# A gated linear attention and MLP kernel: four batches side by side on partition quarters, 32x32 transposes on VectorE, and an order of issue set by hand

## The chip, the cores and the metric

The kernel runs on one core of a Trainium2 chip. The metric is the device time of one execution in microseconds (us), as a median over runs. Engines: PE is TensorE, PEld its weight loads, DVE is VectorE, ACT is ScalarE, POOL is GpSimd, SP is the engine whose queue issues most DMAs.

## The reference

Four batches, eight heads, 768 tokens, 48 dimensions per head, in float32. A gated linear attention is followed by an MLP with a SoLU activation and a layer norm:

```python
for t in range(S):
    state = alpha[:, :, t, :, None] * state + einsum('bhd,bhe->bhde', k[:, :, t], v[:, :, t])
    y[:, :, t] = einsum('bhd,bhde->bhe', q[:, :, t], state)
x = y.transpose(0, 2, 1, 3).reshape(B * S, H * D)          # 3072 x 384
h = x @ w_in                                                # 3072 x 1024
e = exp(h - h.max(-1));  sm = e / (e.sum(-1) + 1e-9)
solu = h * sm
ln = (solu - mean) / sqrt(var + 1e-6) * g_ln
out = ln @ w_out                                            # 3072 x 384
```

The weights arrive as float64, and the kernel converts them to float32 itself.

## The kernel before

Both kernels cut the tokens into chunks of 128, 24 in all. In each chunk the decays become products by two scans along time (one backward for the keys, one forward for the queries). For that alpha, q and k must lie with the dimensions on the partitions and time along the row. The old kernel transposes them on PE, two heads to a matmul, and ACT copies the result out:

```python
    def transposed(src, dst):
        tp = ps_tp.tile([P, NP, P], FP, tag="tp", name="tp")
        for j in range(NP):
            nc.tensor.transpose(out=tp[:, j], in_=src[:, 2 * j : 2 * j + 2, :], identity=ident)
        nc.scalar.copy(out=dst, in_=tp)
```

The scores of a chunk are 8 matmuls with 48 rows each, in two row strips. What is read from the state and what comes from the scores are summed in four column strips of 32:

```python
        for j in range(NP):
            for i in range(2):
                nc.tensor.matmul(a[i][:, j], lhsT=d["kT"][heads[i], j], rhs=d["qT"][heads[i], j], ...)
        # ... reading the state, h being the head, r the column strip
        mm(a, r, states[b][:, h // 2, h % 2], d["qT"][:, h // 2])
```

The loop issues one chunk of attention, one up-projection (`up`, two halves, with exp on ACT and the product on DVE after each) and one output projection (`down`) in every round. The order of its instructions on each engine is not the order of the text: a scheduler moves them.

The fast path must prove that the weights were in range. So both kernels fetch the weights a second time, one piece a chunk, and ACT takes sums of it:

```python
    def in_range(i):
        raw = fetch(i)                                   # DMA, on SP's queue
        sq = wtmp.tile([P, raw.shape[1]], FP, tag="sq", name="sq")
        nc.scalar.activation(out=sq, in_=raw[:, :, 1].bitcast(FP), func=AF.Square, accum_out=far[:, i, 0:1])
        nc.scalar.activation(out=sq, in_=sq, func=AF.Exp, scale=-(2.0**24), accum_out=far[:, i, 1:2])
```

## Time and profile before

| | before |
|---|---|
| time, median of 3 runs | 464.62 us (464.06 to 465.41) |
| span of the profiled run, granted PE clock | 462.2 us, 0.971 |
| PE busy | 90% |
| first output projection starts | 96.5 us |
| one period on PE (one chunk) | 16.74 us, so 66.9 for four |

The prediction below shows the lines that carry this.

### The profile page before, as it was taken

The page shows a single profiled execution, that of the slowest core. Times are in us where ns is not written, and L with a number is a line of the kernel's source. Part 1 is how long each engine was busy: PE and PEld are TensorE (multiplying, and loading weights), DVE is VectorE, ACT ScalarE, POOL GpSimd, SP SyncE. Part 2 cuts the span into 40 slices and gives each one's busy share as a digit, 9 for nine tenths or more (in the row PEclk, how much of TensorE's full clock was granted, in tenths as well). Part 3 has the DMA queues.
Part 4 walks back from the last instruction along what each step waited for, and adds up shares of the span by engine and source line. Part 5 has one row for each costly group of instructions (what it writes and reads, how often), then busy time and mean ns, then how long its engine had stood idle before and what let it go on. Part 6 is the DMA issues. An engine that isn't in the chain of part 4 may idle for free.

```text
span 462.2 us, 9424 instructions
## 1 busy us (share of the span) xinstructions
PE 416.6 (90%) x3827; PEld 341.2 (74%) x3827; DVE 278.0 (60%) x562; ACT 161.9 (35%) x320; POOL 198.8 (43%) x212
## 2 busy tenths in 40 slices
PE   2546848889999999999999999999999999999992
PEld 2336737668878877977987887887797798778761
DVE  5738979996655654764754755665576475454121
ACT  3122335424434538613423332332241242333210
POOL 8435646755334424433524533443442453443120
PEclk9996986999999999999999999999999999999997
DMA  8696449145445549332341332333231100000001
GB/s 185 172 186 152 92 107 178 37 87 132 114 79 118 111 91 272 101 70 36 71 81 27 77 74 47 59 70 70 36 70 34 18 18 18 13 8 19 18 17 43
DMA packets 133477, 37.02 MB, mean 80 GB/s; under 512 B 126504, under 2 KB 129840, under 8 KB 133424
## 3 DMA queue, kind: packets, MB, share of 16 engines
q1 hardware_dynamic: 133120, 36.19, 36.2%
q8 instruction: 32, 0.52, 0.5%
q14 instruction: 21, 0.17, 0.1%
q10 hardware_dynamic: 304, 0.14, 0.1%
HBM read 31.59 MB, written 4.72 MB: 79 GB/s over the span
## 4 chain that ended last, share of the span: by engine, by line
PE 80%; DVE 11%; POOL 6%; issue 1%; ACT 1%; DMA 0%; SPq 0%; POOLq 0%; DVEq 0%; ACTq 0%
PE o L306 27%; PE h L274 26%; PE y L216 7%; PE tp L127 7%; PE a L190 5%; PE kv L248 4%; POOL low L406 2%; PE tp_k L203 2%; PE o L301 2%; DVE top L402 2%; DVE qF L151 1%; DVE power L405 1%; DVE top L399 1%; DVE sT L195 1%; DVE hT L141 1%; DVE w_out L408 1%
## 5 line engine op out<-in xcount | busy, mean ns | idle before, releaser
L274 PE MATMUL h<-xT,w_in 128*128 128x128 f32 x1152 | 141.3, 279 | 12.5 <-POOL w_in L408 7.2
L274 PEld LDWEIGHTS h<-xT,w_in 128*128 128x128 f32 x1152 | 135.9, 195 | 15.0 <-POOL w_in L408 7.8
L306 PE MATMUL o<-w_out,u 128*128 128x385 f32 x384 | 130.7, 492 | 0.9 <-POOL w_out L444 0.5
L306 PEld LDWEIGHTS o<-w_out,u 128*128 128x128 f32 x384 | 70.9, 190 | 46.6 <-DVE w_out L444 1.5
L327 POOL TENSOR_TENSOR r<-sums,mhalf 128x1 f32<-128x1 f32 x24 | 13.2, 551 | 127.7 <-DVE sums L323 127.7
L128 ACT COPY aT<-tp 128x512 f32<-128x512 f32 x24 | 14.0, 585 | 129.6 <-PE tp L127 129.6
L316 DVE COPY sums<-o 128x3 f32<-128x3 f32 x24 | 3.9, 161 | 90.5 <-PE o L306 90.4
L280 DVE TENSOR_TENSOR u<-h,e 128x512 f32<-128x512 f32 x48 | 32.9, 685 | 41.4 <-ACT e L279 41.3
L162 POOL TENSOR_TENSOR qT<-qT,qF 128x512 f32<-128x512 f32 x24 | 28.5, 1188 | 46.5 <-DVE qF L151 41.0
L281 ACT ACTIVATE u<-u 128x512 f32<-128x512 f32 x48 | 30.2, 630 | 48.4 <-DVE u L280 48.4
L279 ACT ACTIVATE e<-h 128x512 f32<-128x512 f32 x48 | 28.6, 596 | 50.1 <-PE h L274 49.7
L289 POOL TENSOR_TENSOR part_e<-e 128x512 f32<-128x512 f32 x24 | 31.2, 1299 | 19.3 <-ACT e L279 19.3
L216 PE MATMUL y<-sT,vn 128*32 128x128 f32 x768 | 29.2, 285 | 11.1 <-DVE sT L195 11.1
L169 POOL TENSOR_TENSOR kT<-kT,hT 128x508 f32<-128x508 f32 x24 | 28.5, 1189 | 17.3 <-ACT kT L128 17.1
L141 DVE TENSOR_TENSOR_SCAN hT<-aT,unit 128x516 f32<-128x516 f32 x24 | 29.6, 1232 | 8.3 <-ACT aT L128 8.2
L190 PE MATMUL a<-qT,kT 48*128 48x128 f32 x384 | 28.8, 291 | 5.9 <-POOL qT L162 5.6
L216 PEld LDWEIGHTS y<-sT,vn 128*32 128x32 f32 x768 | 22.9, 115 | 13.7 <-DVE sT L195 13.3
L195 DVE TENSOR_TENSOR sT<-a,mask 128x512 f32<-128x512 f32 x48 | 30.8, 680 | 0.9 <-PE a L190 0.8
L151 DVE TENSOR_TENSOR_SCAN qF<-aT,seed 128x516 f32<-128x516 f32 x24 | 30.2, 1259 | 1.2 <-DVE seed L149 0.5
L190 PEld LDWEIGHTS a<-qT,kT 48*128 48x128 f32 x384 | 24.1, 193 | 8.9 <-POOL qT L162 5.7
L292 POOL TENSOR_TENSOR part_e<-part_e 128x256 f32<-128x256 f32 x24 | 27.7, 1154 | 1.9
L289 DVE TENSOR_TENSOR part_u<-u 128x512 f32<-128x512 f32 x24 | 18.9, 787 | 15.4 <-ACT u L281 15.4
(85 smaller groups left out, 544.7 us busy)
## 6 DMA issues: line engine op xcount, KB each, us to landing
raw<-in_moe_w_out_dram SPq DMA_DIRECT2D x16, 384.0 KB, 3.9
an<-in_alpha_dram SPq DMA_DIRECT2D x24, 192.0 KB, 2.7
qn<-in_q_dram SPq DMA_DIRECT2D x24, 192.0 KB, 3.3
kn<-in_k_dram SPq DMA_DIRECT2D x24, 192.0 KB, 3.0
out_dram<-o_sb SPq DMA_DIRECT2D x24, 192.0 KB, 2.1
raw<-in_moe_w_in_dram SPq DMA_DIRECT2D x32, 128.0 KB, 3.2
vn<-in_v_dram SPq DMA_DIRECT2D x24, 128.0 KB, 2.5
raw<-in_moe_w_in_dram SPq DMA_DIRECT2D x32, 64.0 KB, 2.7
```

What stands on the lines that cost most here:

```text
L127: nc.tensor.transpose(out=tp[:, j], in_=src[:, 2 * j : 2 * j + 2, :], identity=ident)
L141: nc.vector.tensor_tensor_scan(out=h[:, 0 : NP * SW][:, ::-1], data0=a.rearrange("p j s -> p (j s)")[:, ::-1], data1=unit.rearrange("p j s ...
L151: nc.vector.tensor_tensor_scan(out=d["qF"].rearrange("p j s -> p (j s)"), data0=a.rearrange("p j s -> p (j s)"), data1=s.rearrange("p j s ...
L190: nc.tensor.matmul(a[i][:, j], lhsT=d["kT"][heads[i], j], rhs=d["qT"][heads[i], j], start=True, stop=True)
L195: nc.vector.tensor_tensor(out=d["sT"][:, i], in0=a[i], in1=mask[:, None, :].to_broadcast([P, NP, P]), op=ALU.mult)
L216: nc.tensor.matmul(y[32 * r : 32 * r + 32, a], lhsT=lhsT, rhs=rhs, start=r not in begun, stop=stop, skip_group_check=True, tile_position=( ...
L274: nc.tensor.matmul(h[:, f], lhsT=w_in[:, a, (f0 + f) * P : (f0 + f + 1) * P], rhs=d["xT"][:, a], start=(a == 0), stop=(a == KC - 1),)
L279: nc.scalar.activation(out=d["e"][:, fs], in_=h, func=AF.Exp)
L280: nc.vector.tensor_tensor(out=d["u"][:, fs], in0=h, in1=d["e"][:, fs], op=ALU.mult)
L281: nc.scalar.activation(out=d["u2"][:, fs], in_=d["u"][:, fs], func=AF.Square)
L289: eng.tensor_tensor(out=t, in0=d[key][:, 0:HF], in1=d[key][:, HF:FC], op=ALU.add)
L306: nc.tensor.matmul(o[:, 0 : DM + 1], lhsT=d["u"][:, f], rhs=w_out[:, f], start=(f == 0), stop=(f == FC - 1), skip_group_check=True,)
```

## The change

The intent is to give PE less attention work. One chunk of each of the four batches is done at the same time, each batch on a quarter of the partitions. So there are six groups of four chunks. alpha, q and k are loaded so that DVE's 32x32 transpose finishes them with no matmul and no copy; scores run in four row strips, the state is read with 32x32 tiles in all 16 positions. The diff, cut to its core:

```diff
+    ctx.enter_context(tc.manual_schedule())
...
-    def transposed(src, dst):            # PE and ACT
...
+    def load(g):
+        for src, dst in ((alpha, an), (k, kn), (q, qn)):
+            for b in range(B):
+                nc.sync.dma_start(
+                    out=dst[32 * b : 32 * b + 32].rearrange("t h u d -> t h (u d)"),
+                    in_=src[b, :, t, :].rearrange("h (t u) d -> t h (u d)", u=TQ))
+    def blocks(src, dst, extra):
+        nc.vector.transpose(out=dst.rearrange("p h (t u) -> p h u t", u=TQ), in_=src[:, :, :, 0:E0])
+        nc.vector.transpose(out=extra.rearrange("p j (i t u) -> p u j i t", u=TQ, i=2), in_=...)
...
+    def scores(g, half):
+        for i in range(NP):
+            h = half * NP + i
+            for kb, qb in ((h, h), (H + h // 2, H + h)):
+                for b in range(B):
+                    nc.tensor.matmul(a[b][:, i], lhsT=kT[quarter(b), kb], rhs=qv[quarter(b), qb],
+                                     tile_position=(32 * b, 0), ...)
+    # reading the state
+    mm(b, a, r, 32 * b, state[p, rows + h, e], qv[p, rows + h])        # tile_position=(32 * b, 32 * r)
...
     for m in range(N + DOWN):
+        g, s = m // B + 1, m % B
+            if s == 0:
+                alpha_T(g)
+                for i in range(3):
+                    scan_back(g, i)
+            elif s == 1:
+                for i in range(3):
+                    scan_on(g, i)
         if rise:
             up(m, 0)
         if m > DOWN:
             finish(m - DOWN - 1)
+            s == 0: keys_T, keys, alpha_max, decay      s == 1: queries_T, queries, load(g + 1)
+            s == 2: scores(g, 0)                        s == 3: keys_back(g)
+        if m < DOWN: ... bits(i); add(i)                # conversion of w_out
         if rise:
             up(m, 1)
             partial(m)
+        if attn and s == 3: read_out(g)
         if fall:
             down(m - DOWN)
+        if attn and s == 2: scores(g, 1)
+        if attn and s == 3: next_state(g); load_v(g + 1)
+        if 0 <= m - 6 < len(pieces):
+            in_range(m - 6)
```

`manual_schedule` turns the scheduler off, so every engine now runs its instructions in the order of this text.

## The prediction

> **What bounds the kernel now.** I read the page's busy shares and its slices first, then the chain that ended last, then one period of TensorE's timeline.
>
> ```profile
> PE 416.6 (90%) x3827; PEld 341.2 (74%) x3827; DVE 278.0 (60%) x562; ACT 161.9 (35%) x320; POOL 198.8 (43%) x212
> ...
> PE   2546848889999999999999999999999999999992
> ...
> DVE  5738979996655654764754755665576475454121
> ...
> PEclk9996986999999999999999999999999999999997
> ...
> PE 80%; DVE 11%; POOL 6%; issue 1%; ACT 1%; DMA 0%; SPq 0%; POOLq 0%; DVEq 0%; ACTq 0%
> ```
>
> There are two stages. In the first eight or so slices (11.6 us each) PE is partly idle and DVE is nearly full; from then on PE is full to the end. The chain says the same: PE holds 80% of it, and the DVE and POOL shares are weight conversion and scans at the start. The merged chain in order of time gives the border: the first row below is the first output projection, the second the last one.
>
> ```profile
> 96.49 4.80 PE o L306 x14
> ...
> 448.48 5.31 PE o L306 x16
> ```
>
> So 96.5 us of prologue, about 357 us in which PE sets the pace, and a tail of 8.4 us after 453.8. One period of the steady part, on PE (start, length, line, operation):
>
> ```profile
> 302.29 0.60 PE L127 MATMUL tp<-ident,an 128*128 128x128 f32 x4
> 302.72 0.60 PE L127 MATMUL tp<-ident,qn 128*128 128x128 f32 x4
> 303.16 2.84 PE L274 MATMUL h<-xT,w_in 128*128 128x128 f32 x24
> 305.93 1.16 PE L190 MATMUL a<-qT,kT 48*128 48x128 f32 x16
> 307.02 0.66 PE L127 MATMUL tp<-ident,kn 128*128 128x128 f32 x4
> 307.52 2.84 PE L274 MATMUL h<-xT,w_in 128*128 128x128 f32 x24
> 310.20 0.60 PE L203 MATMUL tp_k<-ident,kT 128*128 128x128 f32 x4
> 310.73 0.86 PE L216 MATMUL y<-qT,state 128*32 128x128 f32 x24
> 311.41 1.06 PE L216 MATMUL y<-sT,vn 128*32 128x128 f32 x32
> 312.39 1.16 PE L248 MATMUL kv<-vn,kg 128*128 128x128 f32 x8
> 313.39 0.28 PE L301 MATMUL o<-ones,sum_e 128*128 128x1 f32 x2
> 313.53 0.36 PE L301 MATMUL o<-ones,sum_u 128*128 128x1 f32 x2
> ```
>
> No row waits for another engine, so a row costs the distance from its start to the next start (the printed lengths overlap). The chain's rows put one period at 16.74 us (320.06 less 303.32). The parts: up-projection 2 x 2.68 = 5.36; output projection 5.29 and its sums 0.36, together 5.65; attention 5.65, of which transposes 0.43 + 0.44 + 0.50 + 0.53 = 1.90, scores 1.09, reading the state 0.68, scores times values 0.98, new state 1.00. Check of this ledger: from 96.5 us the old kernel has 24 output projections (135.6), 21 up-projections (112.6) and 20 chunks of attention (113, less 4 new states never made) to do: 96.5 + 357.2 = 453.7, and the trace has 453.8.
>
> The 24 passes that read the state take 0.68 us, 28 ns each, against 2.68/24 = 112 ns for a pass that fills the array: four column strips run side by side at nearly full gain. The scores use two row strips: 16 in 1.09 us, 68 ns each.
>
> **What the Trainium skill says.** "TensorEngine Tiling (Array Packing)", section Tiling Modes, has 32-row, 32-column and 32x32 tiles run independently, with a drain when the mode changes; the 28 ns and 68 ns agree. "TensorE: Matmul & The Clock Gate", Part 3, gives 10.6 times for 16 tiles, and a few ns from tile to tile; nothing in this trace has 16 tiles. "Vector Engine (DVE) Microarchitecture Reference", section 3.8, sustains one element per cycle per lane in the 32x32 transpose; no transpose of DVE is in this trace. "SBUF — State Buffer", section "SBUF: two separate sides", has DVE and GpSimd exclude each other on a shared port pair. The trace agrees: the same small operation takes 0.16 us when POOL is quiet and 0.82 us when it starts after a POOL operation.
>
> ```profile
> 9.79 0.16 DVE L148 TENSOR_SCALAR least<-hT 128x4 f32<-128x4 f32 x1
> ...
> 305.01 0.82 DVE L148 TENSOR_SCALAR least<-hT 128x4 f32<-128x4 f32 x1
> ...
> 304.98 0.83 POOL L181 TENSOR_TENSOR state<-state,hT 128x384 f32<-128x384 f32 x1 [1.11 <-DVE hT L141]
> ```
>
> **The change part by part, on PE.** The new kernel works in six groups of four chunks (one chunk of each batch). Each matmul is two passes. Per group:
> - Transposes of alpha, q and k leave PE: 4 x 1.37 = 5.5 us. The keys' way back needs 12 transposes where there were 16: 12 x 0.11 + 0.1 = 1.45, before 2.1.
> - Scores: a head's 48 dimensions become 32 and a masked 16, so 64 matmuls, 128 passes. Four row strips at once: 32 rounds of 0.112 = 3.6, with starts 3.9; before 4.4.
> - Reading the state: 128 matmuls of 32x32, 256 passes. In 16 tiles that is 16 rounds of 0.112 = 1.8, estimate 1.9; before 2.7.
> - Scores times values: the same 128 passes in four strips, 32 x 0.11 = 3.5, with starts 3.7; before 3.9.
> - New state: 32 matmuls of 64 columns and 16 of 128, four strips: 16 x 0.056 + 8 x 0.11 = 1.8, estimate 2.0; before 4.0.
> Sum 13.0 us a group against 22.6: 2.4 us less per chunk. A chunk then costs 5.36 + 5.65 + 3.2 = 14.3 us where it cost 16.7, if PE never waits.
>
> **On the other engines.** ACT loses three copies of 0.58 us per chunk. DVE gains six transposes per group, 1024 or 512 elements a lane, an estimate of 1.07 and 0.53 us from the page above, some 5.2 us a group with overheads; it saves a quarter of the scans (six of 1.23 us per group where there were eight) and small state additions. Steady DVE work is near 40 us of a 57 us group: enough on average. But DVE and POOL now do a group's preparation in one lump. The chunks of a group: the first carries alpha's transposes, three backward scans, the keys; the second three forward scans, the queries; the third issues the scores, first half, right after its first up-projection. DVE, from the group's start to the end of the query transposes: state 1.4, alpha 1.8, scans 3.7, keys 1.7, maximum 1.7, up-projection products 3 x 0.69, finishing 2 x 0.64, partial sums 2.0, forward scans with their small operations 7.0, queries 1.7, in all 24.4; POOL then needs 1.2 + 2.4 for the queries: 28 us. PE gets there after two chunks and one up-half, 2 x 11.0 + 2.7 = 24.7. A wait of about 3.4 us a group; without collisions on the shared port (partial 1.35, forward scans 5.2) about 1, with all of them about 6. Four groups (2 to 5) have it in the steady part.
>
> **Prologue.** Here DVE sets the end. Its work up to the last scores of group 1: transposes 10.4, twelve scans 14.8, their small operations 5, maxima 3.4, weight conversion 36 (six pieces of 0.42 + 1.30 + 0.58 us, eight of 0.51 + 0.87 + 0.62, half the additions), sixteen masks at 0.68 = 10.9, products and partial sums 10.2, state 1.1: 92 us. It starts when alpha has landed, about 6.5 us (0.79 MB at the 185 GB/s of the first slice plus 2.7 us), and loses some 5 us while group 0 goes around DVE, POOL and PE: 104. Then PE reads group 1 out (5.6), forms the mean of the output weights (16 passes, 5.2) and waits for the first subtraction (1.5): first output projection at about 116, not 96.5, but with one more up-projection and four more chunks of attention behind it. If conversion runs without collisions it is near 106.
>
> **Sum.** After that: 24 output projections 135.6, 20 up-projections 107.2, attention of groups 2 to 4 3 x 13.0, of the last group without state update 9.5, new state of group 1 2.0, changes of mode and gaps 3, in all 296. With a first projection at 112 (between 106 and 116), waits of 4 x 2.5 = 10 (I take less than 3.4, since an order set by hand was probably tried), and the tail 8.4: 426.4 of span. The time is 2.4 us more than the span before (464.6 against 462.2): 428.8, given as 428.
>
> **The rivals.**
> 1. DVE becomes the bound. For: 92 us in the prologue, 24 in two chunks of 22. Against: 40 of 57 over the group. If its transposes run at half rate, 5 us a group are added in the prologue and before the scores: 10 + 4 x 5 = 30, so 455.
> 2. The 16 tiles don't run side by side, because each pass has its own weight load (PEld is 74% busy). At the 28 ns of four strips the state costs 7.2 in place of 1.9 a group; five groups: +26, so 454. For: nothing here has more than four tiles. Against: starts in a strip group follow within nanoseconds, loads included.
> 3. Nothing waits and the prologue is short: 106 + 296 + 8.4 + 2.4 = 413.
> 4. The transposes' share was hidden and nothing is gained. Against: PE's rows show no wait, and the ledger closes within 0.1 us, so a microsecond off PE is one off the time.
>
> **Range and chances.** Low 408: rival 3 and a little from the prologue. High 450: rivals 1 or 2 nearly in full. For less than 2% gain (above 455.3) both would have to come, or a stall I don't see: faster 0.93, same 0.05, slower 0.02.
>
> **What would show it.** PE's period over four chunks should be 57 to 62 us (66.9 before). The timeline should have no transposes from an, qn or kn; the state's 256 passes in about 2 us, the scores' 128 in about 3.9. The first output projection should start at 106 to 118. A wait of PE's first score of a group for POOL's queries should stand at 1 to 6 us. DVE's 128x1024 transpose should take about 1.1 us. I am wrong if the state's passes stay near 28 ns, if the transposes take 2 us, or if PE waits for DVE at the up-projections too.

## More of the kernel before

One more line helps to compare later. It is the busy time of every engine in a stretch of time (columns: stretch, its length, busy us and instructions of PE, PEld, DVE, ACT, POOL, then granted clock, DMA share, GB/s):

```profile
21.00:96.50 75.50, 51.35 (x407) 43.32 (x407) 61.56 (x103) 27.76 (x52) 43.97 (x39) 0.86 0.58 120
```

Between the first up-projection and the first output projection DVE is busy 61.6 of 75.5 us, 82%.

## The result, and the profile after

The kernel after takes 546.17 us (median of 4 runs, 545.51 to 549.36); before takes 464.34 in the same rounds. The ratio is 1.1765, 95% interval 1.1708 to 1.1822. The result is correct. The prediction of a gain was wrong: the kernel lost 18%.

Busy shares, slices and the chain by engine on the page of the kernel after:

```profile
PE 405.8 (74%) x5007; PEld 329.8 (60%) x5007; DVE 292.1 (53%) x479; ACT 128.6 (23%) x251; POOL 173.2 (32%) x169
...
PE   0028527366899599987689895698796888999993
...
DVE  2998879574159764059624156716245864033411
...
PEclk9999966586989979998888998987999979899997
...
PE 41%; DVE 25%; DMA 12%; POOL 6%; ACT 5%; issue 5%; SPq 4%; DVEq 0%; ACTq 0%; POOLq 0%
```

PE's busy time went down only from 416.6 to 405.8 us, at least in part because some of it ran at a lower clock (0.901 over the run, before 0.971). More important, no engine is full any more. PE has holes from end to end, DVE swings between 9 and 0, and PE holds 41% of the chain where it held 80%. A kernel in which nobody is full and the chain hops among four engines and the DMA queues is bound by waiting.

The chain's rows for the first and the last output projection:

```profile
151.87 7.14 PE o L327 x16
...
533.86 5.31 PE o L327 x16
```

The prologue is 151.9 us (before 96.5, predicted 112), and the stretch after it is 547.6 - 151.9 = 395.7 us (predicted 426.4 - 112 = 314.4). So of the 121 us by which the span missed, 40 lie before the first output projection and 81 after it. One group took 85.1 us, from the up-projection that starts at 232.57 to the one at 317.69.

PE's waits, summed (columns: who waits, for whom, us in total, times, longest):

```profile
PE a L216 <- POOL qv L192: 47.4, 6, 29.1
PE h L295 <- DVE u L301: 45.2, 14, 10.5
PE y L240 <- issue: 12.3, 9, 1.8
PE tp L229 <- DVE sT L221: 11.2, 2, 9.7
```

The wait for the queries (first line) was predicted: apart from one of 29 us at the very start it is 18.3 us in five groups (2.0 us in group 1, 4.1 in each of groups 2 to 5). The second line was not: PE stands 14 times at the up-projection for DVE's product `u`. DVE is only 53% busy, so why is the product late? The merged timeline of all engines answers for one of those places:

```profile
238.40 5.43 PE L327 MATMUL o<-w_out,u 128*128 128x385 f32 x16
239.21 2.19 SPq L385 DMA_DIRECT2D raw<-in_moe_w_in_dram  x4
243.94 0.66 ACT L435 ACTIVATE sq<-raw 128x512 f32<-128x512 f32 x1 [18.52 <-DMA raw<-in_moe_w_in_dram]
...
245.35 0.58 ACT L300 ACTIVATE e<-h 128x512 f32<-128x512 f32 x1
245.97 0.69 DVE L301 TENSOR_TENSOR u<-h,e 128x512 f32<-128x512 f32 x1 [6.31 <-ACT e L300]
...
246.71 0.71 PE L295 MATMUL h<-xT,w_in 128*128 128x128 f32 x4 [2.88 <-DVE u L301]
```

Read it backwards. PE waits 2.88 us for `u`; DVE has waited 6.31 us for the exponential `e`; the up-projection behind `e` had ended at 238, but ACT stood 18.52 us at `sq`, the first instruction of the range check, until its weight piece landed. "Perfetto Trace Analysis", section Tensor Engine Instruction, of the Trainium skill says that ACT, DVE and GpSimd are strict FIFOs; this trace agrees, `e` stood 7 us behind `sq`. And the fetch itself was late: it is issued at 239.21, behind the value loads on SP's queue, which had to wait for their buffer. A little later the same queue shows another such order, with twelve loads ahead of the piece (SP's DMA issues):

```profile
265.24 1.89 SPq L124 DMA_DIRECT2D an<-in_alpha_dram  x4
267.17 3.33 SPq L124 DMA_DIRECT2D kn<-in_k_dram  x4
270.60 2.31 SPq L124 DMA_DIRECT2D qn<-in_q_dram  x4
273.54 3.28 SPq L385 DMA_DIRECT2D raw<-in_moe_w_in_dram  x4
```

A wait could also cost more than its own length. Here are the same 64 score matmuls twice (columns as in the windows above): first a half that PE began without a wait, then the half that began after 4.10 us of waiting for the queries.

```profile
204.80:206.80 2.00, 2.00 (x66) 1.88 (x65) 0.00 (x0) 0.66 (x2) 0.00 (x0) 1.00 0.00 0
269.94:273.67 3.73, 3.73 (x64) 3.50 (x64) 2.35 (x4) 0.63 (x1) 2.88 (x3) 0.50 1.12 203
```

After the wait the granted clock reads 0.50 in place of 1.00, and the matmuls take 3.73 us in place of 2.0. Not every wait did this: the 24 up-projection matmuls that began at 246.71 after 2.88 us of waiting took 2.94 us, about as long as those that began at 296.21 without a wait (2.84).

The transposes took twice what was predicted (groups by form; us in total, mean ns):

```profile
L137 DVE STREAM_TRANSPOSE kT<-kn 128x1024 f32<-128x1024 f32 x6 | 12.3, 2050 | 0.7 <-DMA kn<-in_k_dram 0.6
...
L138 DVE STREAM_TRANSPOSE kT<-kn 128x512 f32<-128x512 f32 x6 | 6.5, 1088 | 0.0
```

And PE's read-out of group 3 with its holes:

```profile
299.82 2.24 PE L240 MATMUL y<-qv,state 32*32 32x128 f32 x150
303.53 1.58 PE L240 MATMUL y<-qv,state 32*32 32x128 f32 x102 [1.47 <-issue]
305.04 1.06 PE L240 MATMUL y<-sT,vn 128*32 128x128 f32 x26
306.98 3.04 PE L240 MATMUL y<-sT,vn 128*32 128x128 f32 x102 [0.88 <-issue]
```

Two holes of 1.47 and 0.88 us are put down to "issue": nothing that the profile shows was missing. Some 0.9 and 1.5 us before the holes begin, at about 301.2 and 304.6 us, the instruction queue moved a packet of 16 KB. Without the hole the first two rows take 2.24 + 1.51 = 3.75 us for 252 of the 256 passes that read the state, where I had predicted 1.9.

### The profile page after: what moved, and what is told of

It reads as the page before. It is cut to its first block, busy times and chain, and to the rows that moved or that the text cites. A ratio compares the mean times of both kernels' runs of the same rounds, so it can differ in the third digit from the quotient of the medians.

```text
span 547.6 us, 11453 instructions
## 1 busy us (share of the span) xinstructions
PE 405.8 (74%) x5007; PEld 329.8 (60%) x5007; DVE 292.1 (53%) x479; ACT 128.6 (23%) x251; POOL 173.2 (32%) x169
## 3 DMA queue, kind: packets, MB, share of 16 engines
q10 hardware_dynamic: 1088, 1.71, 1.6%
## 4 chain that ended last, share of the span: by engine, by line
PE 41%; DVE 25%; DMA 12%; POOL 6%; ACT 5%; issue 5%; SPq 4%; DVEq 0%; ACTq 0%; POOLq 0%
PE o L327 14%; PE h L295 12%; PE y L240 7%; PE a L216 4%; DMA kn<-in_k_dram 4%; DVE aT L157 3%; DMA raw<-in_moe_w_in_dram 3%; DVE u L301 3%; DVE qv L137 2%; DMA raw<-in_moe_w_out_dram 2%; DMA an<-in_alpha_dram 2%; DVE kT L137 2%; POOL low L410 2%; DVE sT L221 2%; PE kv L274 1%
## 5 line engine op out<-in xcount | busy, mean ns | idle before, releaser
L295 PE MATMUL h<-xT,w_in 128*128 128x128 f32 x1152 | 155.0, 299 | 45.2 <-DVE u L301 45.2
L295 PEld LDWEIGHTS h<-xT,w_in 128*128 128x128 f32 x1152 | 149.2, 213 | 55.1 <-DVE u L301 51.0
L216 PE MATMUL a<-qv,kT 32*128 32x128 f32 x768 | 45.3, 383 | 55.5 <-POOL qv L192 47.4
L216 PEld LDWEIGHTS a<-qv,kT 32*128 32x128 f32 x768 | 40.9, 282 | 60.5 <-POOL qv L192 48.6
L283 DVE TENSOR_TENSOR state<-state,kv 128x512 f32<-128x512 f32 x8 | 5.5, 688 | 46.8 <-PE kv L274 46.8
L179 POOL TENSOR_TENSOR kT<-kT,hT 128x1016 f32<-128x1016 f32 (+1 forms) x12 | 20.0, 1689 | 32.0 <-DVE kT L137 32.0
L435 ACT ACTIVATE sq<-raw 128x384 f32<-128x384 f32 (+1 forms) x14 | 8.4, 599 | 86.6 <-DMA raw<-in_moe_w_in_dram 56.9
L240 PE MATMUL y<-qv,state 32*32 32x128 f32 x1280 | 21.5, 278 | 8.1 <-issue 7.9
L240 PEld LDWEIGHTS y<-sT,vn 128*32 128x32 f32 x768 | 22.6, 115 | 6.9 <-issue 6.7
L157 DVE TENSOR_TENSOR_SCAN aT<-aT,seed 128x516 f32<-128x516 f32 x18 | 24.2, 1346 | 0.6
L410 POOL TENSOR_TENSOR low<-low,power 128x384 f32<-128x384 f32 (+1 forms) x14 | 16.2, 1156 | 24.6 <-DVE power L409 15.3
```

The costliest lines, as they stand in the source:

```text
L157: nc.vector.tensor_tensor_scan(out=o, data0=a, data1=s, initial=1.0, op0=ALU.mult, op1=ALU.add)
L216: nc.tensor.matmul(a[b][:, i], lhsT=kT[quarter(b), kb], rhs=qv[quarter(b), qb], start=kb == h, stop=kb != h, tile_position=(32 * b, 0), sk ...
L240: nc.tensor.matmul(y[b][quarter(r), a], lhsT=lhsT, rhs=rhs, start=(b, r) not in begun, stop=stop, tile_position=(row, 32 * r), skip_group_ ...
L295: nc.tensor.matmul(h[:, f], lhsT=w_in[:, a, (f0 + f) * P : (f0 + f + 1) * P], rhs=d["xT"][:, a], start=(a == 0), stop=(a == KC - 1),)
L410: nc.gpsimd.tensor_tensor(out=low, in0=low, in1=power.bitcast(FP), op=ALU.mult)
```

## The experiments

There were 15 runs. The time of the kernel before on the same chip stands beside each result. Runs e1 to e11 are single executions, so their state is unknown; differences under 2 us are not read from them (the kernel before was between 465.0 and 466.3 beside them). The four runs of e12 spread over 4.4 us and those of e15 over 3.2, so the 5 us of e5 and of e9 below are little more than such a spread. e12 to e15 were timed in three rounds. Results are correct unless said otherwise.

### e1 and e2: the range check

e1 leaves the check out (and sets its sums to zero). e2 keeps it, but fetches the piece two chunks before ACT reads it:

```diff
-        if 0 <= m - 6 < len(pieces):
-            in_range(m - 6)
+        if float64 and 0 <= m - 6 < len(pieces):
+            fetch(m - 6, nc.sync)
+        if 0 <= m - 8 < len(pieces):
+            in_range(m - 8)          # without its own fetch
```

> The weight-range checks (14 pieces fetched once more and squared on ACT) are left out, nothing else. Theory A (ACT works in order of issue; a check waits there for its piece, whose transfer stands on the SP queue behind the loads of the next group, and the exponentials behind the check are late, so PE waits): a group of four chunks falls from 85 to 62-68 us, the time from 546 to 470-490 us. Rival B (DVE's slower transposes, 2.05 us in place of 1.07, and the lump of preparation set the group): the group stays above 78 us and the time above 520.

> All checks are made, but each stands on ACT two chunks after its transfer was issued; the transfers stand where they stood. Theory A: within 8 us of e1_nocheck, 470-495 us, with no wait of ACT for a piece over 2 us. If it is the work or the bytes of the checks and not the waiting: near 546.

e1 took 515.31 us and e2 514.23 (before 466.28). So the check costs 31 to 32 us by its waiting and nothing by its work: with all the work kept, but the data there in time, the same 32 us are won. The direction was right, the size too large: e1 lies between what the two theories expected. In e2 a group takes 71.2 us instead of 85.1. The first output projection stays at 152.8: all of this lies after it.

### e3 and e4: the scheduler

e3 takes the `manual_schedule` line out of the kernel after. e4 puts the same line into the kernel before.

```diff
-    ctx.enter_context(tc.manual_schedule())      # e3, from the kernel after
+    ctx.enter_context(tc.manual_schedule())      # e4, into the kernel before
```

> The same program without the hand-set order: the scheduler orders each engine's instructions as it does in the kernel before. Theory A and its twin in the prologue (conversions at ACT's head): 430-480 us, first output projection before 125 us. If the layout itself is what costs (slow transposes, preparation in lumps): above 510.

> The kernel before, with its program order as the order of issue. If an order fixed by hand is costly wherever a check or conversion is waited for at an engine's head: 490-560 us against 464. If the hand order is harmless by itself and only this layout suffers: within 15 us of 464.

e3 took 478.09 and e4 498.98 (before 466.28). One line is worth 68 us in the new kernel: of the 80 us lost (against the 466.28 of these rounds), 68 are the order and 12 the rest. All of the 68 lie after the first output projection: that stretch is 320.7 us in e3 and 395.7 in the kernel after, while the prologue did not get shorter (155.6 and 151.9). It is no fault of the new order alone, because the old kernel's text, run as it is written, also loses 33. PE's waits in e4:

```profile
PE kv L249 <- ACT kg L206: 51.8, 19, 17.8
PE tp L128 <- DMA an<-in_alpha_dram: 20.5, 2, 16.1
```

There the copy of the keys stands in ACT's queue behind a square that waits for DVE, and PE waits for it nearly once a chunk. The scheduler had hidden this. Of the 33 us, 24 lie before the first output projection (at 120.5 us, where it was 96.5). In e3 a group takes 62.7 us, well under the 66.9 of before; what the new layout loses there lies in the prologue (first output projection at 155.6).

### e5: the transposes alone

e5 is e3 with the transposes writing side by side instead of 16 bytes apart. The result is wrong (time order is scrambled), the work is the same.

```diff
-        nc.vector.transpose(out=dst.rearrange("p h (t u) -> p h u t", u=TQ), ...)
+        nc.vector.transpose(out=dst.rearrange("p h (u t) -> p h u t", u=TQ), ...)
```

> The scheduled form of e3_auto, with the transposes' output written contiguously within a block (the order of positions is wrong, so the result is wrong on purpose). If the 16-byte step of the output is what makes a 128x1024 transpose take 2.05 us: 1.1 us each, and the time falls from 478 to 455-468. If the transpose of 4-byte elements runs at half rate whatever the output: 2.0 us and 474-480 us.

```profile
L136 DVE STREAM_TRANSPOSE kT<-kn 128x1024 f32<-128x1024 f32 x6 | 7.4, 1235 | 0.1
...
L137 DVE STREAM_TRANSPOSE kT<-kn 128x512 f32<-128x512 f32 x6 | 4.0, 669 | 0.0
```

The 1024-element transpose goes from 2.05 to 1.24 us and the 512-element one from 1.09 to 0.67. From the two sizes, an element costs (1235 - 669)/512 = 1.1 ns side by side and (2050 - 1088)/512 = 1.9 ns at a step of 16 bytes. The time was 472.66 (before 465.29), only 5.4 us under e3: the output step is the cause of the slow transposes, but in that order of issue slow transposes were no large part of the loss.

### e6: the next group's first DVE work earlier

In the order by hand, alpha's transposes and the three backward scans stood at the start of a group, ahead of the product that PE needs. e6 is e2 with this lump issued at the end of the group before.

```diff
+    def early(g):
+        alpha_T(g)
+        for i in range(3):
+            scan_back(g, i)
...
-            if s == 0:
-                alpha_T(g)
-                for i in range(3):
-                    scan_back(g, i)
...
             up(m, 1)
             partial(m)
+            if attn and s == 3 and g + 1 < G:
+                early(g + 1)
```

> e2_checklate, with the alpha transposes and backward scans of the next group moved to the last chunk of the group before, where DVE is idle. Theory C (the lump of DVE work in a group's first two chunks makes PE wait for the queries, 4.1 us, and the products, 1.7 us): those two waits go, PE's clock stays up in between, the group falls from 71.2 to 62-66 us, the time from 514 to 485-495. If DVE's lump is not it: 71 and 514.

493.73 us (before 465.29), 20.5 less than e2, as expected. A group takes 67.6 us in place of 71.2, more than the 62 to 66 expected. So a lump on DVE did stop PE by standing ahead of shorter work in the same queue: PE's wait for the product (1.5 to 1.7 us a group in e2) is gone, and its wait for the queries falls from 4.1 to about 2.7.

### e7: the conversion of the output weights off the head of the queues

e7 is e6 with the conversion after the partial sums, its last multiplication on DVE instead of ACT, and more buffers for it.

```diff
-    two = pool("two", 4)
+    two = pool("two", 8)
...
-            nc.scalar.mul(out=dst, in_=dst, mul=g_col[:, c : c + 1])
+            nc.vector.tensor_scalar(out=dst, in0=dst, scalar1=g_col[:, c : c + 1], scalar2=None, op0=ALU.mult)
```

> e6_early, with the conversions of the output weights behind the exponentials of their chunk, and their gain multiplied by DVE in place of ACT. Theory A in the prologue (ACT's head waits for a piece's way around DVE and POOL while an exponential stands behind it): first output projection at 120-138 us in place of 152, time 460-480. If DVE's sum of work sets the prologue: first projection above 145 and within 8 us of e6_early.

494.89 us, nothing won; the first output projection is at 151.0, in e6 at 149.9. This was a miss, and the rival's numbers. In the prologue ACT does not hold the others up as it does with the range check; but the edit also gives DVE eight multiplications, which could hide a gain of a few microseconds.

### e8: the holes at the read-out

e8 is e7 with the read-out cut into three parts, put between halves of the up- and output projections. It also moves the keys' way back from a group's fourth chunk to its second, which the cut below leaves out. The amount of work is the same.

```diff
+            elif s == 3:
+                read_out(g, 0)        # state, first half
         if rise:
             up(m, 1)
             partial(m)
-            read_out(g)
-            down(m - DOWN)
+            read_out(g, 1)            # state, second half
+            down(m - DOWN, 0)
+            read_out(g, 2)            # scores times values
+            down(m - DOWN, 1)
```

> e7_conv, with the read-out cut in three and up- and output projections between the parts. Theory D (some 256 small matmuls in a row use up PE's instructions faster than they are fetched, gaps of 1-2 us marked issue, twice a group): the issue gaps fall from 3 us a group to under 1, the time by 8-16 us against e7_conv. If the gaps are anything else, or the changes of tiling cost as much: within 5 us of e7_conv.

483.37 us (before 465.29), 11.5 less than e7. PE's waits marked issue at the read-out, 11.8 us in e7, are gone, which is about what was won; no run takes the move of the keys' way back alone. The timeline has no hole left in these stretches, and a clean measure of the state passes:

```profile
204.92 1.90 PE L243 MATMUL y<-qv,state 32*32 32x128 f32 x128
206.75 2.94 PE L300 MATMUL h<-xT,w_in 128*128 128x128 f32 x24
```

128 passes take 206.75 - 204.92 = 1.83 us, 14.3 ns each. The holes appear where several hundred short passes follow each other, and vanish when long ones lie between. That instructions could not be brought fast enough fits this and the packets of the instruction queue, but no run shows it directly: e8 has such packets too, at about 206.5 and 210.9 us, without a hole.

### e9, e10, e11: what the prologue is made of

e9 is e8 with the conversion's passes batched (all of a round's first steps, then all additions, these on DVE) so that DVE doesn't wait for POOL at each piece. e10 is e8 with the scheduler back on. e11 is e8 with the output weights made by one ACT copy, with none of the eight pieces' work on DVE and POOL; its result is wrong.

```diff
+            for i in mine:                    # e9: a second loop
                 add(i)
-            eng = nc.vector if i % 2 else nc.gpsimd
+            eng = nc.vector if kind or i % 2 else nc.gpsimd
-    ctx.enter_context(tc.manual_schedule())   # e10
+        if i >= NIN:                          # e11
+            nc.scalar.activation(out=words(i)[0], in_=lo, func=AF.Copy, scale=2.0**-32)
+            return
```

> e8_inter, with the bit work of a chunk's two or three output-weight pieces ahead of their additions, and all these additions on DVE, so that DVE no longer waits for POOL once per piece (14 us of such waits in e8). Theory E (the prologue is long because DVE, ACT and POOL pass each piece around one after another): first output projection at 135-142 us in place of 149, time 467-478. If the prologue has another bound: within 4 us of 483.

> e8_inter's program, ordered by the scheduler. If the scheduler's prologue and the cut read-out add up: 460-472 us, below e3_auto (478) and e8 (483). If the scheduler undoes the cuts or the gain is the same time twice: 475-482.

> e8_inter, with the output weights made by one ACT copy per piece (wrong result on purpose): no DVE or POOL work for them. It tells how much of the prologue is conversion and how much the preparation of two groups. Theory E: first projection at 110-125 us, time 445-462. If preparing the groups alone holds PE: above 135 and 470.

e9 took 478.19, e10 482.40 and e11 457.33 (before 464.96 for all three). e9 won 5.2 us, just outside its expectation. In e10 the cuts of e8 do not add to what the scheduler does, but not because they don't work there: the issue waits at the read-out fall from 15.3 us (e3) to 1.9, while the first output projection comes at 171.2 us (155.6 in e3) and PE's wait for the mean of the weights grows from 8.3 to 22.6. e11 won 26 us, and this was a hit: its first output projection came at

```profile
124.64 2.86 PE o L340 x8
```

instead of 149.0. So the conversion of the output weights sets the prologue's end. e11 doesn't part the engines: from 10 us to the first output projection DVE is busy 14.0 us less than in e8 and POOL 11.1 less, and DVE's idle time falls by 10.4. That DVE's own work counts there is shown by e15 below.

### e12 and e13: two misses

By now 13 us were missing to the kernel before, so I tried the largest remaining wait of the steady part. e12 is e9 with the first half of the scores issued later, when POOL has finished the queries. e13 is e12 with group 1's loads ahead of three weight pieces on SP's queue.

```diff
-            elif s == 2:                      # e12: from before up(m, 1) ...
-                scores(g, 0)
+        if attn and s == 2:                   # ... to after it
+            scores(g, 0)
+    load(1)                                   # e13
     for i in range(6, 9):
         fetch(i, nc.sync)
-    load(1)
```

> The kernel of e9 with the first half of the scores issued after the second up-projection of its chunk, in place of before it. The theory that what is left in the steady part is waiting for GpSimd's queries with the clock going down meanwhile (3 us a group and about 2 us of cold scores, in four groups or so) expects the wait of the first score to vanish in groups 2 to 5 and the time at 456 to 466 us. The rival, that the masks of the scores then stop PE at the output projection or the second half instead, expects 474 to 480.

> e12, and the loads of group 1 are put on their queue ahead of three weight pieces that wait for a free buffer. The theory that VectorE stands 10 us at the second alpha transposes behind those pieces, and that VectorE sets the end of the prologue, expects another 4 to 10 us less than e12 and a first output projection 4 to 10 us earlier. If the weight pieces are what the prologue waits for in the end, nothing is gained, or a little lost.

e12 took 482.49 us (480.01 to 484.41; before 464.99; ratio 1.0391, 1.0345 to 1.0436), above what either theory expected; the first output projection moved from 144.0 to 148.3 us. PE's waits in e9 and, after it, in e12:

```profile
PE a L216 <- POOL qv L192: 32.4, 2, 29.7
PE h L300 <- DVE u L306: 14.7, 3, 10.2
...
PE a L216 <- POOL part_e L315: 8.9, 3, 3.1
```

```profile
PE a L216 <- POOL qv L192: 29.3, 1, 29.3
PE h L300 <- DVE u L306: 24.9, 8, 10.2
PE a L216 <- DVE sT L221: 23.5, 3, 20.4
```

The waits for POOL in the steady part are gone, as wanted. In their place PE now waits 1.8 to 3.1 us at one up-projection in each of four groups (8 times in all where it was 3). The trace of one of them, at 246.4 us, names the queries again: ACT stands 3.07 us at their multiplication, which waits for POOL, and the exponential that PE needs stands behind it. So the wait only moved to the next instruction of PE; the stretch after the first output projection is 2.5 us shorter (329.9 against 332.4). And in the prologue, where the same line of code also acts, the second half of the scores waits 20.4 us for masks that now stand behind the weight conversion.

e13 took 479.56 us (ratio 1.0318, 1.0293 to 1.0343), 2.9 less than e12, which is within the spread of e12's own runs, with the first output projection at 149.4 instead of 148.3. Its reason was misread. I had taken a wait of 9.9 us of DVE's alpha transpose for "raw" to be that of group 1. The timeline has it at 11.5 us: it is the first transpose of all, waiting for the first load. A sum in the view of waits doesn't say where in the run it lies; the timeline does.

### e14 and e15: the prologue in order, and transposes side by side

e14 is e13 with the prologue's order changed. Both halves of group 1's scores come before the last three weight pieces are converted, the mean of the output weights is summed as pieces come, and its subtraction goes ahead of group 2's DVE work.

```diff
+        if attn and s == 2 and g == 1:
+            scores(g, 0)
+            scores(g, 1)
+            mean(range(2 * FC // DOWN))
         if m < DOWN: ... bits(i); add(i)
...
         if m == DOWN:
-            read_out(g, 2)
-            centre()
+            mean(range(2 * FC // DOWN, FC))
+            centre()
+            early(g + 1)
+            read_out(g, 2)
```

e15 is e14 with a load for groups 1 to 5 that puts the 32 rows of a block side by side in time, so that e5's fast transpose gives the right result. The price is 16 loads with rows of 192 bytes for each of alpha, k and q where there were 4 with rows of 768.

```diff
+                    for u in range(TQ):
+                        nc.sync.dma_start(
+                            out=dst[32 * b : 32 * b + 32, :, u],
+                            in_=src[b, :, g * P + 32 * u : g * P + 32 * u + 32, :].rearrange("h t d -> t h d"))
...
+        o1, o2 = ("p h (u t) -> p h u t", "p j (u i t) -> p u j i t") if g else (
+            "p h (t u) -> p h u t", "p j (i t u) -> p u j i t")
```

> e13 with the prologue's order changed: both halves of the scores of group 1 before the last three weight pieces are converted, the mean of the output weights formed as pieces come and subtracted before VectorE takes up group 2, and the last part of the read-out after the mean. The theory that the prologue is VectorE's work plus waits that the order makes expects the first output projection at 131 to 138 us (149 in e13) and the time 11 to 18 us less, 462 to 469. The rival, that the work itself fills the prologue, expects under 4 us.

> e14, and from group 1 on the loads put the 32 rows of a block side by side, so that the transposes write side by side too and the result stays right (16 loads of 192-byte rows for each of alpha, k and q where there were 4 of 768-byte rows). The 1024-element transpose goes from 2.05 to about 1.24 us, 3.6 us of VectorE per group. If VectorE still sets the prologue, 3 to 7 us less than e14: 456 to 465. If the smaller rows make the loads late, nothing is gained or some lost.

| | time | before | ratio, 95% interval | first output projection |
|---|---|---|---|---|
| e13 | 479.56 us | 464.99 | 1.0318, 1.0293 to 1.0343 | 149.4 us |
| e14 | 470.16 us (468.88 to 471.22) | 465.21 | 1.0106, 1.0077 to 1.0136 | 138.5 us |
| e15 | 457.95 us (456.51 to 459.69) | 465.21 | 0.9842, 0.9804 to 0.9881 | 132.9 us |

e14 won 9.4 us and moved the first output projection by 10.8. That is a little less than expected and far over the rival's 4: somewhat over a quarter of the gap between 149 us and the 112 us predicted was mere order. e15 won 12.2 us more, twice what was expected: 5.7 in the prologue, and the rest after it, where PE's waits for DVE at the up-projection fall from 8.6 us to 2.0. e15 gives the right result and is faster than the kernel before, by 1.6%, an interval clear of 1. The busy shares, slices and chain on its page:

```profile
PE 377.8 (83%) x5007; PEld 305.1 (67%) x5007; DVE 282.5 (62%) x491; ACT 124.0 (27%) x243; POOL 168.0 (37%) x165
...
PE   0007873435999999999999999999999999999992
...
PEclk9999898675999999999998999999999999999998
...
PE 42%; DVE 33%; DMA 6%; ACT 6%; SPq 5%; issue 3%; POOL 3%; ACTq 0%; DVEq 0%
```

From the eleventh slice on PE is full again, at nearly full clock, as it was before. The chain still hops, though PE's waits there are short; I take it that the chain follows the last releaser however short the wait. What holes are left lie in the first ten slices.

## Why the prediction was wrong

What held. PE was the bound before, and a microsecond off PE counts when PE is full: in e15 PE is full and a group takes 62.6 us where four chunks took 66.9. The new state's passes (predicted 2.0 us a group, measured 1.90), the keys' way back (1.45, 1.31) and scores times values (3.7, 3.67 in e15) were right, and so were the scores where PE doesn't stop among them (3.9, 1.99 + 2.00 in e3). The first score's wait for POOL's queries was there, 4.1 us in each of groups 2 to 5 and so inside the 1 to 6. DVE's work in a group was right too: near 40 us predicted, 103.55 us in 163 in e15, which is 39.8 a group. And DVE's work counts at the end of the prologue (e15).

**The step that failed** is one of the sum: "waits of 4 x 2.5 = 10 (I take less than 3.4, since an order set by hand was probably tried)". I added up busy times per engine and allowed for one wait. That wait alone took 16 us (4 x 4.1). And each engine's queue is a line in which one late instruction stops all behind it; with no scheduler, the text's order decides who stands ahead. In place of 10 us the order cost 68 (e3 against the kernel after). Experiments name two parts: 32 us from the range check at the head of ACT's queue (e1, e2) and 20 from alpha's lump on DVE (e6). The other 16 are not parted. The 11 from the read-out in one piece (e8) are a cost besides, which the scheduler leaves: e3 still has 15.3 us of such waits. I had seen `manual_schedule` in the diff, but gave the order no rival of its own. "A stall I don't see" had to share 7% with the rest.

**After the first output projection**, 81 us were missing to the prediction. e2 takes that stretch from 395.7 to 359.6 us, e8 to 332.6 (481.6 - 149.0), and e15 to 323.2 (456.1 - 132.9). Against the 314.4 predicted, which had 10 us of waits in it, 9 are left. Seven of them can be work that I had sized too small, the state's passes, 1.8 us in each of four groups. One group of e15, from 264.93 to 327.49, is 62.6 us long (predicted 57 and 2.5 of waits; 66.9 before):

```profile
294.24 2.07 PE L225 MATMUL a<-qv,kT 32*128 32x128 f32 x64
...
302.70 3.84 PE L225 MATMUL a<-qv,kT 32*128 32x128 f32 x64 [0.57 <-DVE sT L230]
306.47 2.94 PE L309 MATMUL h<-xT,w_in 128*128 128x128 f32 x24
309.35 1.91 PE L252 MATMUL y<-qv,state 32*32 32x128 f32 x128
311.18 2.94 PE L309 MATMUL h<-xT,w_in 128*128 128x128 f32 x24
314.06 1.91 PE L252 MATMUL y<-qv,state 32*32 32x128 f32 x128
```

From start to start: the two halves of the scores take 1.99 and 3.77 us, 5.8 in place of 3.9; the state 2 x 1.83 = 3.7 in place of 1.9. The second half is slower by waits that the row hides: the two halves share four PSUM banks, DVE masks these one after another from 301.96 to 304.44, and a narrow timeline has two passes each starting at 302.70, 303.30 and 303.90 behind them. From 304.8 on, 24 passes start in every 0.4 us. In the group before, the clock adds to it: 0.69 from 240.5 to 246 us, and 4.74 us for the same half. The state's passes are 14.3 ns apart where I had 7: rival 2 half came true. More than four tiles do run together, since four strips needed 28 ns a pass and a full pass takes 112, but the gain stops at 8 times.

**Before it**, 40 us were missing. Here are the windows of the kernel after, prologue and rest:

```profile
10.00:57.00 47.00, 16.36 (x355) 14.67 (x359) 42.63 (x52) 10.11 (x16) 18.70 (x13) 1.00 0.71 140
57.00:152.00 95.00, 53.83 (x754) 48.28 (x747) 60.22 (x84) 22.76 (x42) 35.94 (x34) 0.77 0.37 73
152.00:539.00 387.00, 335.01 (x3904) 266.55 (x3904) 187.27 (x327) 95.14 (x192) 112.97 (x114) 0.93 0.26 56
```

DVE began at 10.1 us (predicted 6.5, though the two terms given there, 0.79 MB at 185 GB/s and 2.7 us, make 7.0), did 42.6 + 60.2 = 103 us of work (predicted 92, which ends at the last scores, so the two compare only roughly), and was idle for 39 of the 142 us to the first output projection, where I had 5 of waits and 12 for PE's last steps. So 4 us are the late load, 11 are work, and some 22 are waits; the last 4 come from my taking 112 where the sum had said 116. Of the work, 8 are the transposes: the twelve of two groups took 6 x 2.05 + 6 x 1.09 = 18.8 us for 10.4. That is rival 1 as a fact, but it is worth 12 us (e15 against e14, five of the six groups) and not the 30 that the rival added (which, added to 428, make 458 and not the 455 written there). Two of the three signs that I had named for being wrong came true: the transposes took 2 us, and PE waited for DVE at the up-projections. The third did not: the state's passes took 14 ns and not 28. In the second window DVE is busy 63% of the time, at a clock of PE of 0.77; e15 has 66.4 of 80 us (83%), as much as the kernel before had in its own prologue.

**"Enough on average"** was the other weak reason. I wrote that DVE had 40 us of work in a 57 us group and that this was enough. It was (e15), once short products no longer stood behind long lumps. An average tells whether an order exists in which nothing waits, not whether the given order is one.

What is settled: order, not work, cost most of the 82 us (68, e3). By hand the way from 546 to 458 us went in steps, each run built on the one before: 31.9 us won (e2), 20.5 (e6), -1.2 (e7), 11.5 (e8), 5.2 (e9), -4.3 (e12), 2.9 (e13), 9.4 (e14) and 12.2 (e15). Only the last cuts work, DVE's in the transposes; e7 and e9 move some from ACT and POOL to DVE. What is not settled: why the passes of the state are 14 ns apart, what exactly the holes called "issue" are, and what the last 21 us of prologue (132.9 against 112) would take.

## What to carry to other kernels

When a diff turns a scheduler off, the order of issue is the first suspect: run the same kernel with the scheduler on, and the old one with it off, before reading any mechanism into the rest. In an order by hand, an instruction that waits for a DMA must not stand ahead of work that PE needs on the same in-order engine; fetch it some rounds earlier. And sum busy times by engine only to see what is possible; for the time, follow each queue through one period and ask what stands at its head.

## What the Trainium skill lacked or had wrong

- "Vector Engine (DVE) Microarchitecture Reference", section 3.8, gives one element per cycle per lane for the 32x32 transpose. With rows written side by side an element took 1.1 ns; with a 16-byte output step, which is what a batched transpose of interleaved rows asks for, 1.9 ns (2.05 us for 1024 elements against 1.24). The section doesn't mention the output step. Section 5.2 of the page does, for other operations (1.71 to 2.51 ns a column where only the output steps with every element), but neither for a step of 16 bytes nor for the transpose.
- "SBUF — State Buffer", section Door 1: The DMA port swizzle, has a note on 16-byte lines: two accesses per line are needed for full bandwidth, and yet 4 fp32 are called free to stride. A step of exactly 4 fp32 is one access per line, and here it was not free for DVE's writes: 2.05 us against 1.24. The first half of the note agrees with the runs; the second, if it means a step of 4, does not.
- "TensorE: Matmul & The Clock Gate", Part 3, gives 10.6 times for 16 tiles; the page's table of advice adds that this is for 512 columns. With 128 columns in float32 and a weight load for every pass, the passes were 14.3 ns apart (3.67 us for 256), 8 times faster than a full pass of 112 ns. The page has no figure for 16 tiles with so few columns.
- "Runtime: NRT & Kernel Launch", section Instruction fetch mechanics, calls the cost of fetching the next 16 KiB of instructions mostly hidden; no page says what a long run of short passes does. Here it had holes of 1.47 and 0.88 us at the read-out, put down to nothing but issue, which interleaving longer passes removed (11.5 us in e8). Whether they are fetching is not shown.
- "Perfetto Trace Analysis", section Tensor Engine Instruction, states the strict FIFO in half a sentence. Its cost in a kernel ordered by hand was 32 us from one kind of instruction (e2), and nothing there warns of a check whose data comes late.
